# Which queue brings the first loads of a one-core kernel, and in what order

## The chip, the cores and the metric

The kernel runs on one core of a Trainium2 chip. The metric is the device time of one execution in microseconds (us); before the change the median of three runs is 621.21 us (621.16 to 621.39).

## The reference

The input x has 2048 rows of 640 numbers. Each row is normalised (mean 0, variance 1). The normalised rows xn go two ways:

- a sliding, dilated attention with 32 heads of 20 numbers: `qkv = xn @ wqkv`; each position looks at itself and at the 7 positions 2, 4, ..., 14 rows before it; softmax over these eight, weighted sum of v, then `@ wo` gives s;
- a feed-forward layer: `silu(xn @ w1) @ w2` with 1536 inner columns, and g = silu of that.

The output is `x + s * g`, all in float32.

## The kernel before

The rows are worked in four groups (two halves of the sequence, even and odd rows), each of four tiles of 128 rows. Every float32 factor is split in a rounded high half and a low half (the rest), and each product is made of three matmuls: high x with high weight, low x with high weight, high x with low weight. For a weight, ScalarE makes the high half from the raw load (L410) and VectorE or GpSimd subtracts to get the low half (L413). The products of q, k and v are made in four quarters of the columns, each from five chunks of 128 rows of wqkv; a chunk of a quarter is called a weight here, and weights 0 to 4 belong to the first quarter, 5 to 9 to the second. Seven weights can stand converted at a time (RING).

The order of the work is found when the program is written, by a planner (class Weave). Each operation is put down with its engine, an assumed duration, what it reads and writes, and a priority (the lower number goes first). TensorE's operations keep the order in which they are put down; on the other engines the planner takes whatever can start first by its own clock, and of several the lowest number. Within one engine the instructions then run in that fixed order. Loads and stores carry bytes; the planner reckons their landing with RATE, LAND and EARLY, and lets LANES = 8 be out in a queue. An operation with `lock=True` excludes another of that kind on VectorE and GpSimd in the planner's clock.

The first quarter of the first group (`first_quarter`) is written out by hand, since here everything still has to arrive:

- TensorE first makes 22 transposes of the identity (L627), which depend on no load, then the transposes of tile 0 (`turn(0)`, L654), three more transposes of the identity, and then the products (L676) in a listed order, in which the transposes of tiles 1 to 3 stand between products.
- The statistics of a tile (L639, L640), its square root on ScalarE (L453), the reciprocal (L455) and the scaling (L644) come ahead of its transposes. Behind them ScalarE copies the transposed tile out as its high half (L658), and VectorE subtracts to get its low half (L662). When a tile's products are done ScalarE evacuates them (L525, L528).
- All loads go through SyncE's queue, in the order of their numbers: tile 0 in two halves of 320 columns (L685), weight 0 (two transfers, L376 and L377), tile 1 (number 2, L439), weights 1 to 5, tile 2 (7), weight 6, tile 3 (8).
- The low halves of weights 2, 3 and 4 are made on VectorE (ON_DVE, number LOW_AT = 3), those of 0, 1 and 5 to 9 on GpSimd.

Of the kernel before, what the change touches and what calls it, by code (L numbers as in the profile page):

```python
# [14 lines left out]
P = 128  # L15
S, D, F, H, DH = 2048, 640, 1536, 32, 20
W = 8
BQ = 192
DC, FC = D // P, F // P
NQ = 4  # L20
HQ = H // NQ
CQ = HQ * DH
J = 8
T = 4
# [8 lines left out]
LO = 10  # L33
LATE = 4.0
# [2 lines left out]
B = 32  # L37
NB = P // B
RUN = D
X_AT = 2, 7, 8  # L40
TILE_AT = 1, 1.5, 2, 2.5
LOW_AT = 3
ON_DVE = (2, 3, 4)


def win(ap, n, step):
# [15 lines left out]
class Weave:  # L62
# [8 lines left out]
    LANES = 8  # L71
    RATE = 310e3
    LAND = 1.9
    EARLY = 10.0, 0.6
    TABLE = 1.28
    PATIENCE = 1.8
    SOFT = 2.5
# [60 lines left out]
    def order(self):  # L138
        engines = ("PE", "POOL", "DVE", "ACT", "SP")
        free = dict.fromkeys(engines, 0.0)  # L140
        can = {e: [] for e in engines}
        tensor = [o for o in self.ops if o.eng == "PE"]
        at = 0
        lock = dma = 0.0
        lanes = {e: [0.0] * self.LANES for e in ("SP", "POOL")}
        table = held = None
        for o in self.ops:
            if o.left == 0:
                can[o.eng].append(o)
        done = []  # L150
        while len(done) < len(self.ops):
            best = None
            for e in engines:
                if e == "PE":
                    c = [tensor[at]] if at < len(tensor) and tensor[at].left == 0 else []
                else:
                    c = can[e]
                if not c:
                    continue
                f = free[e]  # L160
                est = [max(f, o.ready, lock if o.lock else 0.0, lanes[e][0] if o.nbytes else 0.0) for o in c]
                if e == "ACT":
                    est = self.held_back(c, est, table, tensor, at, free["PE"])
                m = min(est)
                if best is None or m < best[0] or (m == best[0] == lock and held == best[1].eng):
                    pick = min((o for o, t in zip(c, est) if t <= m + 1e-9), key=lambda o: (o.prio, o.seq))
                    if pick.prio >= 140:
                        soon = [(t, o.prio, o.seq, o) for o, t in zip(c, est)
                                if o.prio < 100 and t <= m + min(self.PATIENCE, pick.dur * 0.6)]
                        if soon:  # L170
                            m, _, _, pick = min(soon, key=lambda v: v[:3])
                            if best is not None and m >= best[0]:
                                continue
                    best = m, pick
            t, o = best
            e = o.eng
            o.start = t
            dur = o.dur
            if e == "ACT" and o.table is not None and o.table != table:
                table = o.table  # L180
                dur += self.TABLE
            free[e] = t + dur
            if o.nbytes:
                dma = max(dma, t + dur) + o.nbytes / self.RATE
                o.end = dma + self.LAND + o.late + (self.EARLY[1] if lanes[e][-1] and t < self.EARLY[0] else 0.0)
                lanes[e] = lanes[e][1:] + [o.end - o.late]
            else:
                o.end = t + dur
                if o.lock:
                    lock, held = o.end, e  # L190
            if e == "PE":
                at += 1
            else:
                can[e].remove(o)
            done.append(o)
            for u in o.users:
                u.left -= 1
                hop = self.HOP if u.eng != e or o.nbytes else 0.0
                if u.eng == "ACT" and e == "DVE" and u.prio > 0:
                    hop = self.SOFT  # L200
                u.ready = max(u.ready, o.end + hop)
                if u.left == 0:
                    can[u.eng].append(u)
        self.span = max(o.end for o in done)
        return sorted(done, key=lambda o: (o.start, o.seq))
# [7 lines left out]
def local_attention_silu_ffn(ctx: ExitStack, tc: tile.TileContext, x, wqkv, wo, w1, w2, out):  # L213
    nc = tc.nc
# [6 lines left out]
    add = wv.add  # L221
# [6 lines left out]
    def rows(view, g):  # L228
        h, par = groups[g]
        return view[h, :, par::2, :]  # L230
# [64 lines left out]
        add("PE", dur, fn, reads, writes)  # L295
        clock[0] += dur

    def dma(fn, reads, writes, nbytes, prio, dur=0.45, late=0.0):
        add("SP", dur, fn, reads, writes, prio, nbytes=nbytes, late=late)

    clock = [0.0]

# [49 lines left out]
    def raw_load(k):  # L352


        if k >= len(fresh):
            return
        i = fresh[k]
        u = units[i]
        n = width(u)
        if k < DC:  # L360
            r, kr = PR.rearrange("p t w m -> p (t w m)")[:, k * n:(k + 1) * n], [PRK[k]]
        elif k < early:
            s = (k - DC) % 6
            r, kr = (RAW[s], [("raw", s)]) if s < 2 else (G[:, s - 2, :], [("g", s - 2, 0), ("g", s - 2, CA)])
            r = r[:, :n]
        else:
            s = (k - early) % 4
            r, kr = (RAW[s][:, :n], [("raw", s)]) if s < 2 else (XR[s - 2][:, :n], [("xr", s - 2)])
        raws[i] = r, kr
        if u[0] == "q":  # L370
            _, q, c = u
            w = qcols(q)
            all3 = wqkv[c * P:(c + 1) * P, :].rearrange("p (s m) -> p s m", s=3)

            def go():
                nc.sync.dma_start(r[:, :w], all3[:, 0, q * BQ:q * BQ + w])  # L376
                nc.sync.dma_start(r[:, w:].rearrange("p (s m) -> p s m", s=2), all3[:, 1:, q * CQ:(q + 1) * CQ])  # L377
            dma(go, [], kr, n * P * 4, 1 + k if k < 2 * DC else clock[0] + 5, dur=0.9,
                late=0.2 * k if k < 2 * DC else 0.0)
            return  # L380
        elif u[0] == "w1":
            src = w1.rearrange("(c p) f -> p c f", p=P)[:, :, u[1] * P:(u[1] + 1) * P]
            dst = r.rearrange("p (c f) -> p c f", c=DC)
        else:
            m = wo if u[0] == "wo" else w2
            src, dst = m[u[1] * P:(u[1] + 1) * P, :], r
        dma(lambda: nc.sync.dma_start(dst, src), [], kr, n * P * 4, 1 + k if k < 2 * DC else clock[0] + 5)

    def w_load():
# [16 lines left out]
        if not k:  # L406
# [5 lines left out]
        eng, cost, by = ("POOL", po(n), nc.gpsimd) if pool_does else ("DVE", dv(n), nc.vector)  # L412
        add(eng, cost, lambda: by.tensor_tensor(  # L413
            out=r[:, n:2 * n], in0=raw, in1=r[:, :n].bitcast(F32), op=OP.subtract), [kh] + kr, [kl],
            due if pool_does else LOW_AT if k < LO else 50, lock=True)
        if what[i] == "store":
            kept = dram.tile([P, 2 * n], F32, name="half_" + "_".join(map(str, u)))
            halves[u] = kept
# [19 lines left out]
    def load_x(g, t, n=1, prio=None):  # L438
        dma(lambda: nc.sync.dma_start(XIN[:, t:t + n], rows(xg, g)[:, t:t + n]), [],  # L439
            [("xin", u) for u in range(t, t + n)], n * P * D * 4, clock[0] if prio is None else prio,  # L440
            late=LATE if g else 0.4 * t)

    def ln_stats(t, after=()):
        st = ST[t % 2]
# [176 lines left out]
    def first_quarter(i):  # L621
# [45 lines left out]
        def products(t, steps):  # L667

            o, kp = ps[t]
            for k, c in steps:  # L670
                x, kx = (TL, "tl") if k == 1 else (TH, "th")
                wh, wl, kh, kl = ws[c]
                w, kw = (wl, kl) if k == 2 else (wh, kh)
                first, last = t not in given, given.get(t, 0) == 3 * DC - 1
                given[t] = given.get(t, 0) + 1
                pe(mm(512), lambda x=x, c=c, w=w, first=first, last=last: nc.tensor.matmul(  # L676
                    o, x[i][:, c, tsl(t)], w, start=first, stop=last), [(kx, i, c, t), kw], [kp])

        def passes(*ks):
            return [(k, c) for k in ks for c in range(DC)]  # L680

        given = {}
        for k in range(2):
            cs = slice(k * 320, (k + 1) * 320)
            dma(lambda cs=cs: nc.sync.dma_start(XIN[:, 0, cs], rows(xg, 0)[:, 0, cs]), [],  # L685
                [("xin", 0) if k else ("xin", 0, "a")], P * 320 * 4, 0)
        for k, p in enumerate(X_AT):
            load_x(0, k + 1, prio=p)
        for k in range(RING):
# [7 lines left out]
            ps[t] = b, kp  # L697
        turn(0)
        pe(0.11 * WARM2, lambda: warm(WARM2, ACC[5]), [], [("acc", 5)])
        products(0, [(0, 0), (1, 0), (0, 1), (1, 1), (2, 0), (0, 2), (1, 2)])  # L700
        turn(1)
        products(0, [(2, 1), (0, 3), (1, 3), (2, 2)])
        products(1, [(0, 0), (0, 1), (0, 2)])
        products(0, [(0, 4), (1, 4)])
        products(1, [(0, 3), (0, 4)])
        products(0, [(2, 3), (2, 4)])
        products(1, passes(1, 2)[:-3])
        turn(2)
        products(1, passes(2)[-3:])
        products(2, passes(0, 1, 2)[:-3])  # L710
        turn(3)
        products(2, passes(2)[-3:])
        products(3, passes(0, 1, 2))
        wv.writer["first"] = wv.ops[-1]
        w_done(DC)
        return ps
# [262 lines left out]
```

## Time and profile before

| | |
|---|---|
| median of three runs | 621.21 us |
| the profiled execution | 621.44 us |
| its span, first to last instruction | 619.7 us |
| TensorE busy (matmuls) | 614.2 us, 99% |
| VectorE busy | 561.3 us, 91% |
| ScalarE busy | 309.5 us, 50% |
| GpSimd busy | 112.8 us, 18% |

The profile is one execution, recorded by the hardware. PE is TensorE (PEld its weight loads), DVE is VectorE, ACT is ScalarE, POOL is GpSimd, SP is SyncE; a q behind it means its queue of issues. Times count from the first instruction. A row of the timeline gives the start, the length, the engine, the line of the kernel, the operation with its tiles, and how many instructions stand merged in it; in brackets is the idle time in front of it and what ended it. The length of a matmul holds the way through the array, so matmuls that follow one another overlap; their pace is read from their starts. The share of busy time is a mean over the whole span; what a change in the first 25 us does is read from that stretch.

### The profile page before, as it was taken

The page shows a single profiled execution, that of the slowest core. Times are in us where ns is not written, and L with a number is a line of the kernel's source. Part 1 is how long each engine was busy: PE and PEld are TensorE (multiplying, and loading weights), DVE is VectorE, ACT ScalarE, POOL GpSimd, SP SyncE. Part 2 cuts the span into 40 slices and gives each one's busy share as a digit, 9 for nine tenths or more (in the row PEclk, how much of TensorE's full clock was granted, in tenths as well). Part 3 has the DMA queues.
Part 4 walks back from the last instruction along what each step waited for, and adds up shares of the span by engine and source line. Part 5 has one row for each costly group of instructions (what it writes and reads, how often), then busy time and mean ns, then how long its engine had stood idle before and what let it go on. Part 6 is the DMA issues. An engine that isn't in the chain of part 4 may idle for free.

```text
span 619.7 us, 9092 instructions
## 1 busy us (share of the span) xinstructions
PE 614.2 (99%) x3357; PEld 555.3 (90%) x3357; DVE 561.3 (91%) x581; ACT 309.5 (50%) x651; POOL 112.8 (18%) x168
## 2 busy tenths in 40 slices
PE   8999999999999999999999999999999999999997
PEld 7889999998889999999888999999888999998997
DVE  6558999999989997999998999999979999899974
ACT  5435558937376213951944502583396316152750
POOL 4510000011101133111212233311121213311100
PEclk9999999999999999999999999999999999999999
DMA  8999999866999998764699999855579998956642
GB/s 248 343 287 324 354 345 391 356 236 186 304 322 348 328 356 259 238 195 139 203 242 251 340 333 304 276 176 163 169 202 278 251 334 277 316 179 202 206 124 103
DMA packets 65449, 162.45 MB, mean 262 GB/s; under 512 B 7053, under 2 KB 29165, under 8 KB 65405
## 3 DMA queue, kind: packets, MB, share of 16 engines
q0 software_dynamic: 20016, 82.58, 44.6%
q1 hardware_dynamic: 45389, 79.29, 40.6%
q8 instruction: 26, 0.43, 0.3%
q14 instruction: 18, 0.15, 0.1%
HBM read 109.55 MB, written 34.16 MB: 232 GB/s over the span
## 4 chain that ended last, share of the span: by engine, by line
PE 98%; SPq 1%; DMA 0%; DVE 0%; issue 0%
PE acc L766 22%; PE acc L768 15%; PE acc L737 10%; PE acc L739 10%; PE acc L738 10%; PE rot L883 9%; PE rot L884 9%; PE rot L882 9%; PE acc L676 2%; PE rot L768 1%; DMA pr<-in_A_wqkv_dram 0%; PE rot L766 0%; SPq L376 0%; PE acc L864 0%; SPq L377 0%; PE rot L654 0%
## 5 line engine op out<-in xcount | busy, mean ns | idle before, releaser
L739 PE MATMUL acc<-w,th 128*128 128x512 f32 (+1 forms) x300 | 112.4, 375 | 0.0
L738 PE MATMUL acc<-w,tl 128*128 128x512 f32 (+1 forms) x300 | 112.4, 375 | 0.0
L737 PE MATMUL acc<-w,th 128*128 128x512 f32 (+1 forms) x300 | 112.4, 375 | 0.0
L766 PE MATMUL acc<-w,sh 128*128 128x384 f32 x384 | 111.7, 334 | 0.0
L768 PE MATMUL acc<-w,sh 128*128 128x256 f32 x384 | 107.1, 279 | 0.0
L888 ACT ACTIVATE sh<-rot 128x512 fp32r<-128x512 f32 x48 | 28.6, 597 | 154.2 <-PE rot L884 154.2
L884 PE MATMUL rot<-th,w 128*128 128x512 f32 x240 | 93.8, 391 | 0.0
L883 PE MATMUL rot<-tl,w 128*128 128x512 f32 x240 | 93.8, 391 | 0.0
L882 PE MATMUL rot<-th,w 128*128 128x512 f32 x240 | 93.5, 389 | 0.0
L571 DVE TENSOR_TENSOR pr<-q,kv 128x2560 f32<-128x2560 f32 x32 | 90.2, 2819 | 1.2 <-DMA raw<-in_A_wqkv_dram 1.0
L609 DVE TENSOR_TENSOR pr<-e,kv 128x2560 f32<-128x2560 f32 x32 | 90.3, 2823 | 0.7
L574 DVE TENSOR_REDUCE l<-pr 128x128 f32<-128x2560 f32 x32 | 90.1, 2815 | 0.5
L614 DVE TENSOR_TENSOR pr<-pr 128x1280 f32<-128x1280 f32 x64 | 74.0, 1156 | 1.5
L402 POOL DMA_DIRECT2D w<-half_w x72 | 38.5, 534 | 190.1 <-PE acc L768 94.0
L766 PEld LDWEIGHTS acc<-w,sh 128*128 128x128 f32 x384 | 72.1, 188 | 1.1
L768 PEld LDWEIGHTS acc<-w,sh 128*128 128x128 f32 x384 | 72.2, 188 | 0.9
L402 POOL DMA_DIRECT2D w<-half_q x52 | 27.6, 531 | 238.8 <-PE rot L884 113.5
L737 PEld LDWEIGHTS acc<-w,th 128*128 128x128 f32 x300 | 56.3, 188 | 8.6
L739 PEld LDWEIGHTS acc<-w,th 128*128 128x128 f32 x300 | 56.3, 188 | 8.6
L738 PEld LDWEIGHTS acc<-w,tl 128*128 128x128 f32 x300 | 56.3, 188 | 8.6
L487 ACT ACTIVATE xin<-sf 32x256 f32<-32x256 f32 (+1 forms) x144 | 54.6, 379 | 9.7 <-DVE sf L514 8.0
L766 PE MATMUL acc<-w,sl 128*128 128x384 f32 x192 | 56.1, 332 | 0.0
(104 smaller groups left out, 1059.5 us busy)
## 6 DMA issues: line engine op xcount, KB each, us to landing
w<-half_w POOLq DMA_DIRECT2D x72, 640.0 KB, 6.1
w<-half_q POOLq DMA_DIRECT2D x39, 512.0 KB, 4.3
half_w<-w SPq DMA_DIRECT2D x24, 640.0 KB
w<-half_wo POOLq DMA_DIRECT2D x15, 640.0 KB, 5.6
kv<-kv SPq DMA_DIRECT2D x15, 560.0 KB
half_q<-w SPq DMA_DIRECT2D x15, 512.0 KB
kv<-kv SPq DMA_DIRECT2D x15, 420.0 KB
gate<-in_B_w_dram SPq DMA_DIRECT2D x16, 320.0 KB
```

The source lines that it names most:

```text
L571: dve(2560, lambda t=t: nc.vector.tensor_tensor(out=PR, in0=win(qq[:, t:t + 2, :], W, 0), in1=win(kv[:, 0, t:t + 2, :], W, CQ), op=OP.mult ...
L574: dve(2560, lambda t=t: nc.vector.tensor_reduce(out=l[:, t:t + 2].rearrange("p t w h -> p (t w h)"), in_=PR.rearrange("p t w (h d) -> p (t ...
L609: dve(2560, lambda t=t, v=v: nc.vector.tensor_tensor(out=PR.rearrange("p t w (h d) -> p t (w h) d", d=DH), in0=e[:, t:t + 2].rearrange("p ...
L614: dve(2 * k * CQ, lambda k=k: nc.vector.tensor_tensor(out=PR[:, :, 0:k, :], in0=PR[:, :, 0:k, :], in1=PR[:, :, k:2 * k, :], op=OP.add), [] ...
L737: nc.tensor.matmul(o, hi, wh, start=c == 0, stop=False)
L738: nc.tensor.matmul(o, lo, wh, start=False, stop=False)
L739: nc.tensor.matmul(o, hi, wl, start=False, stop=c == DC - 1)
L766: nc.tensor.matmul(a[t][0][:, :CA], st, w[:, :CA], start=first, stop=last)
L768: nc.tensor.matmul(b[t // 2][0][:, h * CB:(h + 1) * CB], st, w[:, CA:], start=first and h == 0, stop=last, skip_group_check=True)
L882: nc.tensor.matmul(h, wh[:, cs], TH[i][:, c, :], start=c == 0, stop=False)
L883: nc.tensor.matmul(h, wh[:, cs], TL[i][:, c, :], start=False, stop=False)
L884: nc.tensor.matmul(h, wl[:, cs], TH[i][:, c, :], start=False, stop=c == DC - 1)
```

## The change

ScalarE's queue now issues the second half of tile 0 and both transfers of weight 0; SyncE's queue issues the rest, in the order first half of tile 0, tile 1, weights 1 to 4, tiles 2 and 3, weights 5 and 6. The low halves of weights 1, 2, 3, 5 and 6 are made on VectorE, those of 0, 4 and 7 to 9 on GpSimd; for weights 1 to 3 the number is 1.9, ahead of the statistics of tile 2 (number 2), and a low half of that number now gives way to an operation with a lower number that can start soon. The numbers by which the planner reckons early landings are changed, and ScalarE's queue gets eight lanes in its clock. The list of TensorE's steps is written as a string (h: high x, high weight; x: low x, high weight; w: high x, low weight; T: transposes of a tile).

```diff
-X_AT = 2, 7, 8
+X_AT = 0, 5.5, 5.6
-LOW_AT = 3
-ON_DVE = (2, 3, 4)
+LOW_AT = 1.9, 1.9, 1.9, 1.9, 2.6, 3
+ON_DVE = (1, 2, 3, 5, 6)
+FIRST = """0h0 0x0 0h1 0x1 0w0 0h2 0x2 T1 0w1 0h3 0x3 0w2 1h012 0h4 0x4 1h34 0w34 1x01234 1w01 T2 1w234
+           2h01234 2x01234 2w01 T3 2w234 3h01234 3x01234 3w01234"""
...
-    EARLY = 10.0, 0.6
+    EARLY = 8.0, 0.2, 350e3
...
-        lanes = {e: [0.0] * self.LANES for e in ("SP", "POOL")}
+        lanes = {e: [0.0] * self.LANES for e in ("SP", "POOL", "ACT")}
...
-                    if pick.prio >= 140:
+                    if pick.prio >= 140 or pick.prio == LOW_AT[0]:
                         soon = [(t, o.prio, o.seq, o) for o, t in zip(c, est)
-                                if o.prio < 100 and t <= m + min(self.PATIENCE, pick.dur * 0.6)]
+                                if o.prio < min(pick.prio, 100) and t <= m + min(self.PATIENCE, pick.dur * 0.6)]
...
-                dma = max(dma, t + dur) + o.nbytes / self.RATE
+                dma = max(dma, t + dur) + o.nbytes / (self.EARLY[2] if t < self.EARLY[0] else self.RATE)
...
+            by, queue = ("SP", nc.sync) if k else ("ACT", nc.scalar)
+
             def go():
-                nc.sync.dma_start(r[:, :w], all3[:, 0, q * BQ:q * BQ + w])
-                nc.sync.dma_start(r[:, w:].rearrange("p (s m) -> p s m", s=2), all3[:, 1:, q * CQ:(q + 1) * CQ])
-            dma(go, [], kr, n * P * 4, 1 + k if k < 2 * DC else clock[0] + 5, dur=0.9,
-                late=0.2 * k if k < 2 * DC else 0.0)
+                queue.dma_start(r[:, :w], all3[:, 0, q * BQ:q * BQ + w])
+                queue.dma_start(r[:, w:].rearrange("p (s m) -> p s m", s=2), all3[:, 1:, q * CQ:(q + 1) * CQ])
+            dma(go, [], kr, n * P * 4, -1 if not k else 1 + k if k < 2 * DC else clock[0] + 5, dur=0.9,
+                by=by)
...
-            due if pool_does else LOW_AT if k < LO else 50, lock=True)
+            due if pool_does else LOW_AT[min(k, DC)] if k < LO else 50, lock=True)
...
-            late=LATE if g else 0.4 * t)
+            late=LATE if g else 0.2 * t)
...
-            dma(lambda cs=cs: nc.sync.dma_start(XIN[:, 0, cs], rows(xg, 0)[:, 0, cs]), [],
-                [("xin", 0) if k else ("xin", 0, "a")], P * 320 * 4, 0)
+            by, queue = ("ACT", nc.scalar) if k else ("SP", nc.sync)
+            dma(lambda cs=cs, queue=queue: queue.dma_start(XIN[:, 0, cs], rows(xg, 0)[:, 0, cs]), [],
+                [("xin", 0) if k else ("xin", 0, "a")], P * 320 * 4, -2, by=by)
...
-        products(0, [(0, 0), (1, 0), (0, 1), (1, 1), (2, 0), (0, 2), (1, 2)])
-        turn(1)
-        products(0, [(2, 1), (0, 3), (1, 3), (2, 2)])
-        products(1, [(0, 0), (0, 1), (0, 2)])
-        products(0, [(0, 4), (1, 4)])
-        products(1, [(0, 3), (0, 4)])
-        products(0, [(2, 3), (2, 4)])
-        products(1, passes(1, 2)[:-3])
-        turn(2)
...
+        for step in FIRST.split():
+            if step[0] == "T":
+                turn(int(step[1]))
+                continue
+            t, k, cs = int(step[0]), "hxw".index(step[1]), step[2:]
+            products(t, [(k, int(c)) for c in cs])
```

## Rows read from the trace of the kernel before

**Rows 1.** The chain that ended last, shares of the span by engine.

```profile
PE 98%; SPq 1%; DMA 0%; DVE 0%; issue 0%
```

**Rows 2.** Waits of TensorE, whole span: us in total, times, longest us.

```profile
...
PE acc L676 <- DMA pr<-in_A_wqkv_dram: 0.3, 1, 0.3
```

**Rows 3.** Timeline of TensorE, first quarter: start us, length us, instruction.

```profile
1.38 4.96 PE L627 MATMUL rot<-ident 128*128 128x128 f32 x22 [1.38 <-POOL ident masks.py:199]
6.13 1.21 PE L654 MATMUL rot<-ident,xin 128*128 128x128 f32 x5
...
7.56 0.49 PE L676 MATMUL acc<-w,th 128*128 128x512 f32 x1
8.15 0.50 PE L676 MATMUL acc<-w,tl 128*128 128x512 f32 x1
...
9.64 0.50 PE L676 MATMUL acc<-w,th 128*128 128x512 f32 x1 [0.31 <-DMA pr<-in_A_wqkv_dram]
...
10.22 0.71 PE L654 MATMUL rot<-ident,xin 128*128 128x128 f32 x5
...
11.46 1.32 PE L676 MATMUL acc<-w,th 128*128 128x512 f32 x5
...
12.85 1.07 PE L676 MATMUL acc<-w,th 128*128 128x512 f32 x4
...
15.37 0.76 PE L654 MATMUL rot<-ident,xin 128*128 128x128 f32 x5
```

**Rows 4.** Timeline of VectorE, same stretch.

```profile
4.88 0.80 DVE L644 TENSOR_SCALAR xin<-xin,mv,sd 128x384 f32<-128x384 f32 x2
6.41 0.49 DVE L639 BATCH_NORM_STATS2 st<-xin 128x6 f32<-128x320 f32 x1 [0.73 <-DMA xin<-in_A_x_dram]
...
9.93 1.28 DVE L413 TENSOR_TENSOR w<-pr,w 128x512 fp32r<-128x512 f32 x2
11.26 0.89 DVE L662 TENSOR_TENSOR tl<-rot,th 128x384 fp32r<-128x384 f32 x2
12.07 0.68 DVE L413 TENSOR_TENSOR w<-pr,w 128x512 fp32r<-128x512 f32 x1
```

**Rows 5.** Timeline of ScalarE, same stretch.

```profile
7.66 0.63 ACT L410 ACTIVATE w<-pr 128x512 fp32r<-128x512 f32 x1
8.77 0.29 ACT L453 ACTIVATE sd<-mv,epst 128x1 f32<-128x1 f32 x1 [0.48 <-DVE mv L640]
8.97 1.14 ACT L410 ACTIVATE w<-pr 128x512 fp32r<-128x512 f32 x2
10.74 0.77 ACT L658 ACTIVATE th<-rot 128x384 fp32r<-128x384 f32 x2 [0.63 <-PE rot L654]
...
13.96 0.33 ACT L528 ACTIVATE q<-acc 128x192 f32<-128x192 f32 x1 [1.38 <-PE acc L676]
14.19 0.28 ACT L453 ACTIVATE sd<-mv,epst 128x1 f32<-128x1 f32 x1
```

**Rows 6.** Waits of SyncE's issues up to 16 us.

```profile
SPq L377 <- DMA pr<-in_A_wqkv_dram: 0.7, 1, 0.7
```

**Rows 7.** Timeline of SyncE: the issue behind that wait.

```profile
11.15 0.38 SPq L377 DMA_DIRECT2D gate<-in_A_wqkv_dram  x1
```

**Rows 8.** Windows: stretch, length, busy us (count) by engine, granted clock, DMA share, GB/s.

```profile
2.00:3.00 1.00, 1.00 (x7) 1.00 (x6) 0.00 (x0) 0.24 (x2) 1.00 (x1) 1.00 0.87 297
3.00:4.50 1.50, 1.50 (x9) 1.50 (x8) 1.20 (x3) 0.15 (x1) 0.22 (x1) 1.00 0.61 159
4.50:6.50 2.00, 2.00 (x11) 2.00 (x10) 1.06 (x4) 0.78 (x2) 0.14 (x1) 1.00 1.01 340
6.50:10.50 4.00, 3.59 (x18) 2.54 (x17) 3.23 (x8) 2.62 (x6) 2.43 (x2) 1.00 0.93 247
10.50:14.40 3.90, 3.90 (x20) 3.27 (x19) 3.27 (x8) 2.28 (x7) 1.30 (x1) 1.00 0.98 328
```

**Rows 9.** Timeline of GpSimd: one low half of a weight.

```profile
6.36 1.28 POOL L413 TENSOR_TENSOR w<-pr,w 128x512 fp32r<-128x512 f32 x1 [3.14 <-ACT w L410]
```

More of the change, by code (lines that the diff above doesn't have):

```diff
@@ L296, in pe, with dma @@
         clock[0] += dur
-    def dma(fn, reads, writes, nbytes, prio, dur=0.45, late=0.0):
-        add("SP", dur, fn, reads, writes, prio, nbytes=nbytes, late=late)
+    def dma(fn, reads, writes, nbytes, prio, dur=0.45, late=0.0, by="SP"):
+        add(by, dur, fn, reads, writes, prio, nbytes=nbytes, late=late)
     clock = [0.0]
@@ L699, in first_quarter @@
         pe(0.11 * WARM2, lambda: warm(WARM2, ACC[5]), [], [("acc", 5)])
-        products(0, [(0, 0), (1, 0), (0, 1), (1, 1), (2, 0), (0, 2), (1, 2)])
-        turn(1)
-        products(0, [(2, 1), (0, 3), (1, 3), (2, 2)])
-        products(1, [(0, 0), (0, 1), (0, 2)])
-        products(0, [(0, 4), (1, 4)])
-        products(1, [(0, 3), (0, 4)])
-        products(0, [(2, 3), (2, 4)])
-        products(1, passes(1, 2)[:-3])
-        turn(2)
[L709 to L713, printed above, removed]
+        for step in FIRST.split():
[4 more added lines that the diff above has]
+            products(t, [(k, int(c)) for c in cs])
         wv.writer["first"] = wv.ops[-1]
```

## The prediction

> **What bounds the kernel now.** I read the chain of waits first. The reader is to see that TensorE carries 98% of the span by itself [rows 1]: time can only be won where TensorE stands still. The waits of TensorE come next: apart from the 1.4 us before its first instruction [rows 3] there is one entry, 0.3 us [rows 2], and it lies in the first quarter. After 24 us no wait is listed at all, so whatever the first quarter gains or loses reaches the end of the span unchanged, and nothing later can be won. Then the timeline of TensorE for that quarter [rows 3]. I call the products of the listing t-kind-c (0h2: tile 0, high half times high weight, chunk 2; x is the low half of x, w the low half of the weight), and T0 to T3 the transposes of a tile.
>
> The 22 warm-up transposes run from 1.38 to 6.34, and T0 follows at 6.13 with no idle time noted, although the whole of tile 0 was normalised at 5.68 (4.88 + 0.80) [rows 3, 4]. So T0 is bound by the warm-up, which the change leaves alone, and the first tile has about half a microsecond to spare. 0h0 begins at 7.56, 0x0 at 8.15 (it waits for the low half of tile 0, two steps behind T0), 0h2 at 9.64, T1 at 10.22, T2 at 15.37 [rows 3]. Between 0x0 and 0h2 lie 0h1, 0x1 and 0w0: at 0.227 us each ((1.07 - 0.39) / 3 of the run at 12.85) they take 0.68, and 0.8 with the slower start behind a wait. 8.15 + 0.8 = 8.95, so some 0.7 us are lost in front of 0h2. ScalarE shows why [rows 5]: it stood until 8.77 for the square root of tile 1, whose statistics had waited for the load until 6.41 [rows 4], and converts weight 2 only at 8.97; that ends near 9.59 (0.62 later), and 0h2 begins at 9.64.
>
> **The change part by part.** *The order of TensorE* is the same: I wrote the new list out against the old calls, and all 60 products and four turns stand in the same places. It costs nothing.
>
> *Issue.* Before, SyncE issues one after the other; two issues of a weight take nearly 1 us. Taking three of them to ScalarE brings tile 1 and weights 1 to 4 forward by about three issues, 3 x 0.47 = 1.4 us; tiles 2 and 3, put ahead of weight 5, by some 2.4 us and more, and weights 5 and 6 stand behind both tiles. ScalarE now issues three transfers ahead of its table load; the square root of tile 0 is not due before 4.3, so about 1 us is free there and I cost it at nothing (at worst 0.3 us, if the first tile comes 0.8 late and uses up its spare). Issue isn't all: SyncE's issue at 11.15 stood 0.7 us for an earlier load [rows 6, 7], as it would if eight transfers could be out at a time (the planner's LANES is 8). The planner now counts eight for each queue; if the two queues share eight, the eleventh transfer waits for tile 1. That delays issues by 0 to 0.8 us; I take it as hidden, since the engines still have loads in hand. No row shows two queues issuing at once: between issues side by side (1.4 us won) and one after the other (nothing won) I take the first, since each issue here is timed on its own engine; the other end is a case of the second rival.
>
> *Landing.* The windows [rows 8] give the bytes: 0.30 MB by 3.0, 0.54 by 4.5, 1.22 by 6.5, 2.20 by 10.5. Only from 3.0 to 4.5 were the transfer engines idle (share 0.61); from 4.5 to 10.5 they were busy (1.01, 0.93). The lag from moved to landed: tile 1 completes 0.92 MB, moved at 5.6, and VectorE takes it at 6.41 [rows 4]: 0.8. Weight 4 completes 1.97 MB, moved at 9.5; I take the issue at 11.15 as the one that waits for it [rows 7]: 1.6. For the changed kernel I let the flow of 4.5 to 14.4 (298 GB/s as the mean of three rows) begin at 3.0, with a lag of 0.8: weight 4 at 3.0 + 1.67/0.298 + 0.8 = 9.4, tile 2 (2.29 MB) at 10.5, weight 6 (3.15 MB) at 13.4. The bounds: 340 GB/s throughout gives 9.7 and 12.2 for tile 2 and weight 6; the same flow with the lag of 1.6 gives 11.3 and 14.2; no earlier than before gives 11.15 for weight 4 and 13.4 + 0.8 to 1.6 = 14.2 to 15.0 for weight 6.
>
> The Trainium skill speaks against this part ("DMA: Bandwidth & Descriptors", section "Issuing engines are not separate DMA queues"): transfers of all issuing engines run on the same 16 DMA engines and interleave, so a second issuing engine saves the sequencer's time alone. The busy shares above agree for all but 1.5 us. By that rule taken alone only the idle 0.39 x 1.5 = 0.6 us could come back; its result is the second rival below.
>
> *What earlier weights give.* I followed the planner's rule by hand (earliest start first; a weight's conversion gives way to an operation of low number that can start within 0.6 of its length). ScalarE's order then is: tile 0's two copies, square root of tile 1, weights 1 to 4, tile 1's copies, weights 5 and 6, and only then the evacuation of tile 0 and the square root of tile 2. Steps from rows 5: the next instruction starts at 7.66 behind tile 0's copies, 0.20 after a square root, 0.52 after a conversion (two in 1.14, one in 0.63). So weights 1, 2, 3, 4 convert at 7.86, 8.38, 8.90, 9.42. 0h1 then begins at 8.54 (about as before), 0x1 8.77, 0w0 9.00, 0h2 at 9.05 + 0.2 = 9.23, T1 at 9.69 if tile 1 is ready (square root 7.66, scaling done near 8.9; its statistics now run before tile 0's low half is due). Gain at T1: 10.22 - 9.69 = 0.53; I take 0.5.
>
> *The low halves.* Weight 1 goes from GpSimd to VectorE, weight 4 the other way, 5 and 6 to VectorE. VectorE's pair takes 1.28 and one 0.68 [rows 4], GpSimd's one 1.28 [rows 9]. Weights 5 and 6 are used after 24 us; their 1.36 us lie beside other work, where VectorE has room; if that were gone they would delay tile 3 by as much. Weight 4's low half on GpSimd (9.42 + 0.63 + 1.3 = 11.4) is used at 0w4 near 13.0. Both cost nothing.
>
> *Where it may be given back.* Three gates lie behind the gain, each an in-order engine that now stands on a load. (1) Tile 1's copies stand behind weight 4's conversion. They begin 0.52 after T1 (10.22 to 10.74), so at 10.2, and are used 1.47 after it (1h0, second of the run at 11.46); 0.4 can be spared. Weight 4 has to land by 10.1; 9.4 is in time. (2) VectorE's first statistics of tile 2 stand ahead of tile 1's low halves and weight 3's low half, which 0w3 needs (before: third of the run at 12.85, so 13.30; now 12.80). From landing to done: 0.48 + 0.81 + 0.68 = 1.97 [rows 4], so tile 2 must land by 10.8; 10.5 just does. (3) Square root of tile 2 stands behind weight 6: landing + 0.05 + 0.52, then 0.23 behind tile 0's evacuation (13.96 to 14.19), then 1.18 to T2 (14.19 to 15.37) [rows 3, 5] = landing + 1.98. T2 is due at 14.87; weight 6 at 12.9 keeps the whole gain, at 13.4 none. I take 13.3, between the flow's 13.4 and its faster bound and nearest the flow: T2 at 15.28.
>
> *Sum.* The profiled execution took 621.44 (span 619.70 and 1.74 around it), 0.23 over the median of 621.21. 15.37 - 15.28 = 0.09, rounded to 0.1: 621.34 for such an execution, 621.1 as a median. 0.2% of this kernel is 1.24 us, about what a measurement can tell from no change.
>
> **The rivals.** *Gates open.* If the engines hold 340 GB/s, all three loads are in time (weight 6 at 12.2) and 0.5 remains: 620.7. For it: the row from 4.5 to 6.5 reaches 340. Against it: from 6.5 to 10.5 the share was 0.93 and the rate 247. *Loads no earlier, conversions in front* (the other side): if bytes land as before, weight 6 at 14.4 puts T2 at 16.4, 1.0 late, 622.2; weight 4 at 11.15 puts 1h0 about 1.0 late by itself, and these do not add up, since one delay holds both. It decides from weight 6 at 13.4 on. For it: the busy shares; against it: the idle share from 3.0 to 4.5, and the 328 GB/s of the row from 10.5. With the lag of 1.6 at the late end (15.0) it costs 1.6: 622.8. *The change doesn't do what it says*: the square root of tile 1 is no longer the hold, but the planner's clock is off by what T0 is late; if ScalarE's order is the old one, 0h2 stays near 9.6 and the time at 621.2.
>
> **How the numbers follow.** Forecast (part of the gain kept, 620.9 to 621.5) 0.45; gates open 0.25; loads no earlier 0.2; old order 0.1. The range leaves out the ends of the outer two: 620.6 to 622.2. Faster by over 0.2% would need more than TensorE loses in the quarter: 0.02. Slower by over 0.2% (over 622.45) is the late third of the slower rival: 0.06. Within: 0.92.
>
> **What would show it.** In the changed profile: 0h0 at 7.56 again; 0h2 near 9.2; T1 near 9.7; ScalarE idle in front of the conversion of weight 5 or 6, ended by a load; T2 between 14.9 and 15.5; no wait of TensorE after 24 us. T0 before 6.0, a wait of TensorE past the first quarter, or T2 later than 16 would make the prediction wrong.

## The result and the profile after

The changed kernel takes 623.25 us (median of 17 runs, 621.60 to 625.00), the kernel before 621.47 beside it (17 runs, 620.99 to 623.99): ratio 1.0023, 95% interval 1.0013 to 1.0033. It is slower by 1.4 us by the ratio and by 1.8 by the medians, where 621.1 and a range up to 622.2 were forecast. The profiled execution took 622.66 with a span of 620.9, 1.2 us over the span of before; it lies 0.6 under its kernel's median, so up to 0.6 us of the difference isn't in this profile.

The chain of waits of the kernel after, shares of the span by engine; TensorE no longer carries it alone [rows 1]:

```profile
PE 85%; DVE 6%; DMA 5%; ACT 1%; issue 1%; SPq 1%; ACTq 0%; DVEq 0%
```

The waits of TensorE after (us in total, times, longest). The load that held 0h2 [rows 2] is gone; the last entry is T2, and the middle one lies at 392 us, where before had none:

```profile
PE rot L631 <- POOL ident masks.py:199: 1.4, 1, 1.4
PE acc L763 <- DVE sl L887: 0.6, 1, 0.6
PE rot L658 <- DVE xin L648: 0.3, 1, 0.3
```

The timeline of TensorE after, for [rows 3]. T0 at 6.32, 0h0 7.59, 0x0 8.19, 0h2 (second of the pair at 8.99) at 9.22, T1 at 9.73, T2 at 15.52:

```profile
1.38 4.95 PE L631 MATMUL rot<-ident 128*128 128x128 f32 x22 [1.38 <-POOL ident masks.py:199]
6.32 0.91 PE L658 MATMUL rot<-ident,xin 128*128 128x128 f32 x5
...
7.59 0.49 PE L680 MATMUL acc<-w,th 128*128 128x512 f32 x1
8.19 0.50 PE L680 MATMUL acc<-w,tl 128*128 128x512 f32 x1
...
8.99 0.66 PE L680 MATMUL acc<-w,th 128*128 128x512 f32 x2
...
9.73 0.71 PE L658 MATMUL rot<-ident,xin 128*128 128x128 f32 x5
...
15.52 0.77 PE L658 MATMUL rot<-ident,xin 128*128 128x128 f32 x5 [0.26 <-DVE xin L648]
```

ScalarE after, for [rows 5]: it stands for the loads of weights 4, 5 and 6, and the square root of tile 2 at 14.33 comes behind the last of them:

```profile
10.08 0.63 ACT L414 ACTIVATE w<-pr 128x512 fp32r<-128x512 f32 x1 [0.46 <-DMA pr<-in_A_wqkv_dram]
10.62 0.74 ACT L662 ACTIVATE th<-rot 128x384 fp32r<-128x384 f32 x2
12.67 0.63 ACT L414 ACTIVATE w<-raw 128x512 fp32r<-128x512 f32 x1 [1.30 <-DMA raw<-in_A_wqkv_dram]
13.59 0.63 ACT L414 ACTIVATE w<-raw 128x512 fp32r<-128x512 f32 x1 [0.29 <-DMA raw<-in_A_wqkv_dram]
14.12 0.31 ACT L532 ACTIVATE q<-acc 128x192 f32<-128x192 f32 x1
14.33 0.28 ACT L457 ACTIVATE sd<-mv,epst 128x1 f32<-128x1 f32 x1
```

So far this is the forecast quarter, a little worse: its second quarter starts at 24.24, in the profile of before at 24.14. Of the 1.2 us of the spans it carries 0.1. The other 1.1 us lie behind it, at 376 and 392 us, where two steps of TensorE, from the start of one product to the next, are 0.28 and 0.76 us longer than usual and the restarts behind them some 0.1 each. The second in the timeline of TensorE:

```profile
391.08 0.28 PE L765 MATMUL acc<-w,sl 128*128 128x256 f32 x1
391.95 0.44 PE L763 MATMUL acc<-w,sl 128*128 128x384 f32 x1 [0.59 <-DVE sl L887]
```

VectorE's timeline after shows why:

```profile
370.00 0.89 DVE L451 BATCH_NORM_STATS2 st<-xin 128x6 f32<-128x320 f32 x2 [1.28 <-DMA xin<-in_A_x_dram]
...
374.46 0.89 DVE L451 BATCH_NORM_STATS2 st<-xin 128x6 f32<-128x320 f32 x2 [2.34 <-DMA xin<-in_A_x_dram]
375.38 0.21 DVE L453 BATCH_NORM_AGGREGATE mv<-st 128x2 f32<-128x12 f32 x1
375.51 1.24 DVE L887 TENSOR_TENSOR sl<-sf,sh 128x512 fp32r<-128x512 f32 x2
...
389.75 1.48 DVE L618 TENSOR_TENSOR pr<-pr 128x1280 f32<-128x1280 f32 x1
391.16 0.17 DVE L459 RECIPROCAL sd<-sd 128x4 f32<-128x4 f32 x1
391.25 0.65 DVE L887 TENSOR_TENSOR sl<-sf,sh 128x512 fp32r<-128x512 f32 x1
```

The low halves of the silu (sl), which TensorE needs next, stand behind the statistics of the next group's x at 375.51 and behind a step of the attention at 391.25, and that x is late. SyncE issues its load at 353.13 (346.88 before) because XIN is still in use by the attention's output. That the attention is late because VectorE stood idle earlier is an argument here; e4 and e5 below try it. Two large holes, in the timeline of VectorE after:

```profile
228.57 0.21 DVE L453 BATCH_NORM_AGGREGATE mv<-st 128x2 f32<-128x12 f32 x1
231.67 0.69 DVE L887 TENSOR_TENSOR sl<-sf,sh 128x512 fp32r<-128x512 f32 x1 [2.89 <-ACT sf L886]
232.28 2.81 DVE L578 TENSOR_REDUCE l<-pr 128x128 f32<-128x2560 f32 x1
...
324.05 0.63 DVE L603 TENSOR_REDUCE z<-e 128x32 f32<-128x256 f32 x1 [4.58 <-ACT e L592]
```

and the same place of the first in the kernel before, where the attention's sum fills the time and the low half starts no later:

```profile
228.80 0.21 DVE L449 BATCH_NORM_AGGREGATE mv<-st 128x2 f32<-128x12 f32 x1
228.93 2.77 DVE L574 TENSOR_REDUCE l<-pr 128x128 f32<-128x2560 f32 x1
231.61 0.68 DVE L890 TENSOR_TENSOR sl<-sf,sh 128x512 fp32r<-128x512 f32 x1
```

No line of the diff touches these instructions. Their order is the planner's, and the diff moves the planner's clock: worked out as the kernel does it, the second quarter starts at 24.18 on the planner's clock before (24.14 on the chip) and at 23.12 after (24.24 on the chip). Line 169 holds an attention step back when something of low number can start within 0.6 of the step's length, here 1.69 us. Before, VectorE is free at 232.77 by plan and the low half due at 234.71: 1.94, so the sum goes first. After, it is free at 232.84 and the low half due at 233.64: 0.80, so VectorE is made to wait. On the chip VectorE comes there at 228.8 in both, and the wait is 2.89. To turn one order into the other behind the first quarter, at least 84 operations of VectorE, 49 of ScalarE, 10 of SyncE and 6 of GpSimd have to be moved.

### The profile page after: what moved, and what is told of

Read it like the earlier page. It is cut to its first block, busy times and chain, and to the rows that moved or that the text cites. A ratio compares the mean times of both kernels' runs of the same rounds, so it can differ in the third digit from the quotient of the medians.

```text
span 620.9 us, 9092 instructions
## 1 busy us (share of the span) xinstructions
PE 614.7 (99%) x3357; PEld 554.8 (89%) x3357; DVE 561.1 (90%) x583; ACT 311.0 (50%) x652; POOL 113.0 (18%) x166
## 4 chain that ended last, share of the span: by engine, by line
PE 85%; DVE 6%; DMA 5%; ACT 1%; issue 1%; SPq 1%; ACTq 0%; DVEq 0%
PE acc L763 19%; PE acc L765 13%; PE acc L735 9%; PE acc L736 9%; PE acc L734 9%; PE rot L880 8%; PE rot L881 8%; PE rot L879 8%; DMA xin<-in_A_x_dram 3%; PE acc L680 1%; DVE pr L618 1%; DVE l L578 1%; DVE pr L613 1%; DVE pr L575 1%; DMA raw<-in_A_wqkv_dram 1%
```

## The experiments

Order and start can be exchanged, since both kernels have the same 2532 operations with the same dependences. Each kernel below was timed beside the kernel before (medians of 621.49 to 621.70 in its four sets; single executions from 620.74 to 625.17). The table is read from the timelines of TensorE: the starts of the transposes, the first product of the second quarter (Q2), and from there to the last product of the kernel. These columns are of one profiled execution each: those of e5 and e6 are among the fastest of their kernels, that of e7 is the slowest of its. One of e1's twelve executions took 1826.76 us and isn't in its ratio.

```
kernel                    T0     T1     T2   T2-T1    Q2   Q2 to end   median   ratio to before (95%)
before                   6.13  10.22  15.37   5.15  24.14   591.87
after                    6.32   9.73  15.52   5.79  24.24   592.99    623.25   1.0023 (1.0013-1.0033)
e1 new start, old rest   6.12   9.68  15.93   6.25  24.66   591.87    622.07   1.0005 (0.9996-1.0014)
e2 old start, new rest   6.13  10.12  15.27   5.15  24.00   594.22    623.68   1.0038 (1.0021-1.0056)
e3 planner's 5.1 us      6.27  10.01  16.16   6.15  24.88   593.58    623.81   1.0034 (1.0021-1.0048)
e4 exponential first     6.04   9.37  15.60   6.23  24.32   593.69    623.10   1.0019 (1.0010-1.0028)
e5 three places          6.26   9.99  15.15   5.16  23.85   592.60    622.92   1.0020 (1.0006-1.0033)
e6 low halves first      6.12   9.65  15.51   5.86  24.23   592.27    622.40   1.0014 (1.0006-1.0023)
e7 planner's clock right 6.02   9.40  16.01   6.61  24.77   597.62    624.07   1.0054 (1.0034-1.0073)
e8 gates open            6.10   9.35  14.49   5.14  23.18   594.13    621.14   1.0001 (0.9989-1.0013)
e9 e1, one queue         5.74   9.47  16.02   6.55  24.72   591.87    622.73   1.0001 (0.9988-1.0015)
e10 gates and slack      6.25   9.84  14.97   5.13  23.64   591.88    620.99   0.9985 (0.9974-0.9996)
e11 e10, one queue       6.13   9.68  14.86   5.18  24.13   592.08    621.74   1.0003 (0.9992-1.0014)
e12 slack alone          5.64   9.48  14.96   5.48  23.73   593.04    621.92   0.9997 (0.9982-1.0012)
```

**Start and rest exchanged.** The operations that start ahead of Q2 on the planner's clock (23.1 us in the changed kernel, 24.18 in e2) as they were, all others in the other kernel's order (LATER holds its operation numbers; the edits of this section are shortened, and the comments in them are mine):

```diff
-        for o in self.order():
+        head = [o for o in self.order() if o.start < 23.1]
+        kept = {o.seq for o in head}
+        for o in head + [self.ops[k] for k in LATER if k not in kept]:
             o.fn()
```

> The changed kernel for the first quarter, instruction for instruction; from the second quarter on every engine follows the order of the kernel before. Theory 1 (the time is lost because the written-out order behind the first quarter came out differently, not by the loads and conversions of the first quarter): T2 stays near 15.5, the second quarter starts near 24.25, TensorE waits for nothing at 376 and 392 us, and the time is that of the kernel before plus the 0.1 us of the first quarter: 621.6. Rival 2 (the first quarter's own changes cost it: two queues, a later tile 2, low halves on VectorE, which then runs late to the end): the waits at 376 and 392 us stay, 622.7 to 623.3.

> The mirror image: the kernel before for the first quarter, and from the second quarter on every engine in the order of the changed kernel. Theory 1: the second quarter starts at 24.1 as before, and TensorE loses about 1.2 us near 376 and 392 us behind late low halves of the third group's silu: 622.5 to 623.2. Rival 2: no such waits, 621.4 as before.

The waits of TensorE in e1, and then in e2:

```profile
PE rot L631 <- POOL ident masks.py:199: 1.4, 1, 1.4
PE acc L680 <- ACT th L662: 0.4, 1, 0.4
```

```profile
PE rot L627 <- POOL ident masks.py:199: 1.4, 1, 1.4
PE acc L766 <- DVE sl L890: 0.8, 2, 0.6
PE acc L766 <- ACT sh L888: 0.7, 1, 0.7
PE acc L676 <- DMA pr<-in_A_wqkv_dram: 0.3, 1, 0.3
```

With the old order the stretch behind Q2 takes 591.87 us to the hundredth, though Q2 comes 0.5 us later; with the new order behind the old start the waits at 377 and 393 us are back (x issued at 354.15), with one more at 69 us, which puts e2 0.5 us over the forecast of either theory. Theory 1 holds: the loss behind Q2 is the order's. The start by itself costs 0.4 us by the medians, within their uncertainty, 0.5 in this profile, whose T2 is 0.4 later than expected.

**The planner's clock.** One number of the plan, no instruction:

```diff
-        pe(4.5, lambda: warm(WARM, ROT[0]), ["consts"], [("rot", 0)])
+        pe(5.1, lambda: warm(WARM, ROT[0]), ["consts"], [("rot", 0)])
```

> The changed kernel with one assumption of the planner altered: the warm-up transposes count 5.1 us instead of 4.5. No instruction is added or taken away; the order behind the first quarter then comes out close to that of the kernel before (31 places of VectorE, 14 of ScalarE, 8 of SyncE differ from it), the first quarter shifts in one or two places. Theory 1: the waits at 376 and 392 us are gone, 621.4 to 621.8. Rival 2: the number of the planner changes nothing that matters, 622.7 to 623.3.

and, in another kernel, the last product of the first quarter counted 1.0 us longer:

```diff
         wv.writer["first"] = wv.ops[-1]
+        wv.ops[-1].dur += 1.0
```

> The changed kernel with the planner told that the first quarter ends 1.0 us later (its second quarter then starts at 24.12 by its own clock, 24.24 measured; it had 23.12). The first quarter is the same instruction for instruction; the order behind it differs from that of the kernel before in 40 places of VectorE, 22 of ScalarE, 9 of SyncE. Theory 2a (the order is bad because the planner's clock ran 1.1 us ahead of the chip, and good when it agrees): no wait of TensorE behind 25 us, 591.9 us from the second quarter to the end as before, 621.5 to 622.0. Theory 2b (any other order than the tuned one loses some, whatever the clock): a wait somewhere, 622.5 to 624.

Both are slow, in new places: e3 waits 0.8 us for a low half at 76 us, and in e7 eight evacuations at 56 us stand behind the conversion of a weight that is not there:

```profile
55.43 0.74 ACT L414 ACTIVATE w<-gate 128x640 fp32r<-128x640 f32 x1 [5.87 <-DMA gate<-in_B_w_dram]
56.07 0.42 ACT L529 ACTIVATE kv<-acc 128x320 f32<-128x320 f32 x1
```

Theory 2a finds no support, though its test wasn't exact: e7's plan has Q2 at 24.12, 0.12 from after's profile, but in its own profile Q2 came at 24.77 (e3: 23.33 by plan, 24.88 on the chip). 2b stands as far as three orders can show it: each of the other orders that the planner gave (after's, e3's, e7's) loses somewhere, although the plan shows no gap of TensorE behind Q2 for after's and e7's. The profiled execution of e7 is its slowest (627.83 against a median of 624.07), so the 3.6 us that TensorE stands at 56 are an upper case. They aren't all of the 5.8 us that this execution loses behind Q2. Behind them the granted clock reads 0.50 (1.2 GHz) from 57 to 60 us, and a product of 384 columns starts 0.32 us after the last, where it starts 0.17 after it before the wait; ten such steps cost some 1.5 us (an estimate from these rows):

```profile
57.00:60.00 3.00, 3.00 (x10) 3.00 (x11) 3.00 (x3) 2.44 (x8) 0.00 (x0) 0.50 1.07 379
```

```profile
58.85 0.52 PE L734 MATMUL acc<-w,th 128*128 128x384 f32 x1
59.17 0.52 PE L735 MATMUL acc<-w,tl 128*128 128x384 f32 x1
```

**Where in the order.** In MOVES a pair (k, n) puts operation k ahead of operation n in the changed kernel's list. First one instruction, then three:

```diff
+    # e4: operation 993 (exp) ahead of 1438 (first evacuation)
+MOVES = [(993, 1438)]
+    # e5: also 861 (sum of the attention) ahead of 1113 (low half), 1344 (low half) behind 1011
+MOVES = [(861, 1113), (993, 1438), (1344, 1012)]
```

> The changed kernel with a single instruction of ScalarE moved: the exponential of the scores near 320 us stands ahead of the eight evacuations of the next quarter instead of behind them. Theory 1 in its narrow form (this one place starts the chain: VectorE idles 4.6 us for it, the next group's x is loaded 6 us later, its statistics stand ahead of the silu's low halves): the idle time of VectorE at 324 us goes to under 1 us, the load of x near 353 us is issued some 4 us earlier, the waits of TensorE at 376 and 392 us shrink by at least 1 us together, 621.6 to 622.0. If the one place is not enough (VectorE's other idle time since 217 us holds the load back as well), the waits stay: 622.7 to 623.3.

> The changed kernel with three instructions moved back to where the kernel before has them: one product sum of the attention ahead of the silu's low half at 231 us (VectorE idles 2.9 us there), the exponential ahead of the evacuations at 320 us (4.6 us idle), one low half of the attention's output behind three steps of the attention at 329 us (4.3 us idle in the run with the exponential alone). Theory 1a (these places are the chain that makes the next x late): the load of x that was issued at 353.1 goes out by 349, the waits of TensorE at 376 and 392 us are gone or under 0.3 us together, 621.9 to 622.3. Theory 1b (the lost time has many small sources in the order, and three places don't mend it): 622.7 or more.

In e4 the exponential comes at 320.04 and VectorE's 4.58 us shrink to 0.48, but the time is lost again from 325 to 329 us, where a low half waits for the transposed output, which ScalarE still copies behind the evacuations (from 324.28; from 324.04 in the changed kernel):

```profile
320.49 0.63 DVE L603 TENSOR_REDUCE z<-e 128x32 f32<-128x256 f32 x1 [0.48 <-ACT e L592]
...
329.12 0.69 DVE L476 TENSOR_TENSOR tl<-xin,th 128x512 fp32r<-128x512 f32 x1 [4.28 <-ACT th L475]
```

The load of x stays at 353.4 and so do the waits: my narrow theory fell. In e5 the load goes out at 351.8 only (VectorE has a new hole of 2.2 us at 350), the wait at 376 is gone, the one at 391 stays. So closing holes brings the load forward, by 1.3 us of the 4 that I expected, and takes one of the two waits away; but the holes are tied to one another, and the median, 622.92, lies where 1b had put it. That these holes are the whole chain isn't shown.

**The end of the chain.**

```diff
+    # sl ahead of the statistics, sl ahead of the second pair, sl ahead of an attention step
+MOVES = [(1662, 1698), (1667, 1704), (1697, 1467)]
```

> The changed kernel with VectorE's order altered at the end of the chain alone: the two low halves of the silu ahead of the statistics of the next x at 370 to 377 us, and the last low half at 391 us ahead of one attention step. The x stays late (issued near 353). If the low halves' place behind the late statistics is what TensorE waits for, both waits (0.28 and 0.76 us above the usual step) go, and some 0.2 us of slow restarts with them: 1.0 to 1.2 us less than the changed kernel, 622.0 to 622.3. If the silu or the load itself holds TensorE, the waits stay, 623.0 to 623.3.

Both waits are gone with x as late as ever (353.13), and the median is 0.85 under the changed kernel's and 0.1 over my range, though the intervals of the two ratios overlap. That is what TensorE waited for. A new wait, again for a low half, appears at 405 us (0.27 us idle, a step 0.43 longer than usual) and takes part of it back.

**The three gates of the first quarter.** In e1, gate 1 of the prediction bites: weight 4 lands past 10.1, and tile 1's copies and TensorE wait behind its conversion. ScalarE in e1:

```profile
10.69 0.63 ACT L414 ACTIVATE w<-pr 128x512 fp32r<-128x512 f32 x1 [1.11 <-DMA pr<-in_A_wqkv_dram]
11.23 0.75 ACT L662 ACTIVATE th<-rot 128x384 fp32r<-128x384 f32 x2
```

So the old order was kept behind the quarter and work that needs no load was put ahead of the instructions that stand on one:

```diff
+    # ScalarE: first copy of tile 1 ahead of weight 4, square root of tile 2 ahead of weight 5
+    # VectorE: low half of weight 3 and of tile 1 ahead of tile 2's statistics, tile 2 scaled ahead of tile 3's
+MOVES = [(80, 28), (55, 32), (26, 52), (82, 52), (83, 52), (56, 59), (57, 59)]
```

> The later order of the kernel before, and in the changed first quarter the three instructions that stand on a load moved: tile 1's first copy ahead of the conversion of weight 4, the square root of tile 2 ahead of the conversions of weights 5 and 6, and VectorE's low halves ahead of the statistics of tile 2. If those gates cost the quarter its gain, T2 comes at 14.9 (9.7 + the 5.15 us that lay between T1 and T2 before), the second quarter starts at 23.6 to 23.7 and the time is 0.4 us under that of the kernel before: 620.9 to 621.3. If the weights' loads hold the products instead, T2 stays at 15.3 to 15.9 and the time at 621.4 to 622.1.

T2 follows T1 by 5.14, as before the change (5.15), and Q2 starts 1 us earlier than after's. But the profiled execution gives 2.3 us back behind Q2. Seven of the twelve executions took 620.7 to 621.1 and five 622.5 to 623.3, and the profiled one is of the five. Its waits of TensorE behind Q2:

```profile
PE acc L763 <- DVE sl L887: 1.0, 1, 1.0
PE acc L734 <- ACT q L532: 0.7, 1, 0.7
```

They lie at 74 and 52 us. VectorE had stood 6.3 us for a weight's load at 30 to 36 us and ScalarE 4.4 us at 47 to 51. Four places got slack there:

```diff
+    # statistics (480 to 485) ahead of a low half on a load; a conversion (279) behind the evacuations,
+    # its low half (280) behind two steps; two sl (423, 431) ahead of one step
+MOVES += [(480, 202), (481, 202), (482, 202), (483, 202), (484, 202), (485, 202),
+          (279, 287), (280, 288), (423, 243), (431, 243)]
```

> The kernel with the open gates, and behind the first quarter four places of the old order changed that stood at the limit when the quarter ended 1 us earlier: the statistics of the next tiles 2 and 3 ahead of a low half that waits for its load (VectorE idled 6.3 us there), one weight's conversion behind the eight evacuations at 50 us instead of ahead, its low half behind two attention steps, and the silu's low halves at 72 us ahead of one attention step. If the two waits of TensorE (0.8 us at 52, 1.2 us at 74) are what spent the gain of the first quarter, they go: second quarter at 23.2 to 23.7, no wait behind it, 620.4 to 621.0. If the loads between 25 and 60 us hold TensorE in another place, the wait moves and the time stays at 621.1 to 622.

> The kernel before, its first quarter as it was, with only the four places behind the first quarter changed as in the kernel with gates and slack. If that kernel is faster by its first quarter (0.5 us earlier by the profiles), this one stays at the time of the kernel before within 0.3 us: T2 at 15.2 to 15.4, second quarter at 24.0 to 24.2, 591.9 us behind it, 621.2 to 621.7, and fewer of its runs lie above 622.5. If the slack is the whole gain, 620.7 to 621.1.

e10 is faster than both kernels, than the kernel before by an interval that just clears no change: 620.99 us, ratio 0.9985 (0.9974 to 0.9996). Its TensorE waits for nothing after the first instruction; T1 and T2 in its timeline:

```profile
9.84 0.71 PE L658 MATMUL rot<-ident,xin 128*128 128x128 f32 x5
...
14.97 0.71 PE L658 MATMUL rot<-ident,xin 128*128 128x128 f32 x5
```

From T0 to Q2 e10 takes 17.39 us and e8 17.08, the three kernels with the old start 17.87 to 18.09: some 0.5 us or more is won in the first quarter. The four places without the new start (e12) gain nothing: 621.92, ratio 0.9997. But e12 missed what I expected of it: its warm-up was 0.5 us shorter (T2 at 14.96), and behind Q2, where its order is e10's, TensorE waits 0.5 us for a low half at 130 us, which it doesn't in e10. So the same order can lose 1.2 us in one execution (593.04) and nothing in another (591.88), the intervals of e10 and e12 overlap, and that the slack is what lets e10's gain through is likely and not shown.

**The second queue.**

```diff
-            by, queue = ("SP", nc.sync) if k else ("ACT", nc.scalar)
+            by, queue = "SP", nc.sync
```

(the same for the half tile, and weight 0 put ahead of tile 1 in SyncE's order).

> The first run's kernel (changed first quarter, old order behind it) with the half tile and weight 0 issued by SyncE again, at the same places of the order; nothing else differs. The second queue saves issue time only while eight transfers are not yet out: in the changed kernel SyncE issues its eighth at 2.6 us and stands until 4.1, when the first transfer has landed. If that is all it gives, the ninth issue moves from 4.1 to 4.5 at most, the first tile lands some 0.4 us earlier, T0 stays at 6.1 (the warm-up), T2 between 15.2 and 16.0, and the time is that of the first run within 0.3 us: 621.7 to 622.3. If the second queue brings the loads forward as the prediction had it (1.4 us), undoing it puts weight 4's landing at 11 or later and T2 at 16.5 or later: 622.7 to 623.2.

> The kernel with gates and slack, with the half tile and weight 0 issued by SyncE again. If the second queue is worth nothing, the same as that kernel within 0.3 us: 620.5 to 621.2, T2 at 14.5 to 15.0. If it is worth what the prediction gave it, T2 at 15.5 or later, 621.5 or more.

With one queue the ninth issue comes at 4.59 instead of 3.84 to 4.09, and the first tile's statistics begin 0.3 and 0.4 us earlier (3.51 in e9 for 3.84 in e1, 3.63 in e11 for 4.03 in e10). Both medians miss my range upward: they are 0.66 and 0.75 over those of e1 and e10. By the ratios to the kernel before, e9 is no slower than e1 and e11 is 1.1 us slower than e10, with intervals that overlap; at Q2 e9's profile shows only 0.06, e11's 0.49 (tile 3 at 13.1 instead of 11.9). What the second queue is worth, between nothing and some 1 us, stays open; the later T2 that the 1.4 us of my issue count asked for, 16.5 in e9 and 15.5 in e11, came in neither (16.02 and 14.86).

## Why the prediction was wrong

**The step that failed** stands in its first paragraph: "whatever the first quarter gains or loses reaches the end of the span unchanged, and nothing later can be won." I read "no wait of TensorE after 24 us" as a property of the work, when it was one of that one order. Behind the first quarter 1.1 to 2.3 us could be lost, and were (Q2 to end: 592.99 in after and 594.22 in e2 against 591.87), and with the old order put back the loss was gone (e1: 591.87). The first quarter carries 0.1 of the 1.2 us between the two profiles. A wait of TensorE past the first quarter was among my own signs of being wrong. *The order of TensorE is the same* was true and not enough: I worked out the planner's rule by hand for 16 us, and didn't ask what a clock moved by 1.1 us does to the 600 behind it. None of my rivals lay there, so the chance of 0.06 for slower was far too small.

**T0** was held by the warm-up before, and the first tile's spare half microsecond is used up: the whole tile was normalised at 5.68 before [rows 4] and is at 5.79 + 0.80 = 6.59 after. Its first 384 columns, which the first three transposes need, are done earlier, so T0 lost only 0.2, within the 0.3 that I gave as the worst; the "nothing" of the sum was wrong.

**0h2 and T1**: 9.22 and 9.73 against 9.23 and 9.69. Right.

**The gates** stood where I had put them (the first bites in e1, the third in after), and the price of the third is right. T2 was put at the landing of weight 6 plus 1.98; ScalarE takes that weight at 13.59, which gives 13.54 + 1.98 = 15.52, as measured. What I mis-sized is the spread. One forecast of 15.28 stood for all executions, but T2 - T1 lies between 5.16 and 6.61 in the eight profiles with the changed start and shut gates, and at 5.13 to 5.18 in the three with open ones (5.15, 5.15 and 5.48 with the old start). T2 itself lies between 15.15 and 16.16 in those eight, so that the profile of after came within 0.24 of my number is partly luck. Q2 in after, e1 and e3 to e7 is 24.42 on average (23.85 to 24.88), in before, e2 and e12 23.96 (23.73 to 24.14): on these few profiles the start doesn't gain, it loses some 0.5.

**Issue**: the queues do issue side by side (0.75 and 0.76), but they share what may be out. I had that as a doubt, from the eleventh transfer on and hidden; it bit at the ninth. Three issues of ScalarE and five of SyncE are out by 2.64, and SyncE's next is at 4.09, 1 us after it was free. The longest of the waits of SyncE's issues after, up to 16 us, names the half tile that ScalarE had issued (the other 0.5 us of this row lies at 11.9 and is for a later tile):

```profile
SPq L381 <- DMA xin<-in_A_x_dram: 1.5, 2, 1.0
```

**Landing**: the windows of after [rows 8] give 378 GB/s from 3.0 to 4.5 us instead of 159, so the idle share did come back, and no more. Since e9 and e11, with one queue, have 197 and 190 there, it is the second queue that brings it back:

```profile
2.00:3.00 1.00, 1.00 (x7) 1.00 (x6) 0.00 (x0) 0.82 (x1) 1.00 (x1) 1.00 0.82 214
3.00:4.50 1.50, 1.50 (x9) 1.50 (x8) 0.40 (x1) 0.66 (x2) 0.22 (x1) 1.00 1.03 378
4.50:6.50 2.00, 2.00 (x10) 1.61 (x9) 1.57 (x6) 0.60 (x2) 0.00 (x0) 1.00 1.11 333
6.50:10.50 4.00, 3.87 (x21) 2.89 (x22) 3.70 (x10) 3.32 (x8) 1.27 (x1) 1.00 0.92 258
```

The row of e9:

```profile
3.00:4.50 1.50, 1.50 (x9) 1.50 (x8) 0.95 (x3) 0.00 (x0) 0.23 (x1) 1.00 0.78 197
```

Weight 4 landed at 10.0 and not at 9.4, but not for want of bytes. The rows add up to 1.45 MB by 6.5 us, and at 258 GB/s the 1.97 MB up to weight 4 are moved by 8.5, where my flow had 8.6. The term that was too small is the lag from moved to landed: 1.5 us where I took 0.8 (1.6 stood in the bounds). Whether the landing itself took longer, or bytes of later loads were moved in between, no row here separates.

The Trainium skill's rule that speaks against this part ("DMA: Bandwidth & Descriptors", section "Issuing engines are not separate DMA queues") says that a second issuing engine saves only the time of issuing, since the transfers of all run on the same 16 engines and interleave. The trace agrees as far as it goes: with more transfers out at once the statistics of the first tile begin at 4.10 after, at 3.08 before.

**The low halves** on VectorE cost nothing that shows behind Q2: e1 has all of them and needs the same 591.87 us there.

## What to carry to other kernels

Where a planner writes the order, a change of its numbers is a change of the whole program: compare the two orders of every engine to the end before pricing the lines of the diff, and freeze the order behind the edit when only the edit is to be measured. A profile without waits on the bounding engine says that this order is tuned, not that others are as good. An instruction of an in-order engine that stands on a load is a gate for all behind it: let what needs no load pass first.

## What was not expected of the hardware

The 22 warm-up transposes end at different times though nothing ahead of them differs. In e9 they take 4.43 us instead of 4.95: the step from one transpose to the next falls from 0.213 to 0.109 us at the eighteenth, in after only behind the warm-up. The granted clock of the windows reads 1.00 (2.4 GHz) in all of it, so that column doesn't show what halved the step. T0 lies between 5.64 and 6.32 in these kernels, by what the warm-up takes and by when the first tile is normalised. TensorE in e9:

```profile
1.38 4.43 PE L631 MATMUL rot<-ident 128*128 128x128 f32 x22 [1.38 <-POOL ident masks.py:199]
5.74 0.76 PE L658 MATMUL rot<-ident,xin 128*128 128x128 f32 x5
```

Eight transfers out at once is a limit of this program over both issuing queues, not for each: the ninth issue, at 4.09, goes out when the first of ScalarE's has landed. And where TensorE stood for 3.6 us, in e7, its granted clock was at half for the 3 us behind, so the wait cost more than its length.
